# Operand sums moved from GpSimd to VectorE one by one, a reordered seam, and fourth-stage blocks run in pairs

## The chip, the cores and the metric

One Trainium2 core runs the whole program; the metric is the device time of one execution in microseconds (us). The engines are TensorE (PE in the profile, with its weight loads as PEld), VectorE (DVE), ScalarE (ACT), GpSimd (POOL) and SyncE (SP, which here only issues DMAs). TensorE has 128x128 cells; its results go to PSUM, eight banks that VectorE and ScalarE read and GpSimd does not use here.

## The reference, cut to what matters

```python
X = np.fft.rfft(x, axis=1)                       # x: (8, 3072, 256)
Xr, Xi = (X.real.astype(np.float32), X.imag.astype(np.float32))
Yr = Xr @ w_r - Xi @ w_i + b_r                   # mixing over the 256 channels
Yi = Xr @ w_i + Xi @ w_r + b_i
Yr = np.sign(Yr) * np.maximum(np.abs(Yr) - lam, 0.0)      # and Yi alike, lam = 0.01
y = np.fft.irfft(Y, n=x.shape[1], axis=1)
h = y.reshape(B * S, D) @ w_in                   # 256 -> 2048
g = np.where(h >= 1, h, np.where(h <= -1, 0.0, (h + 1) ** 2 / 4))
return g @ w_out                                 # 2048 -> 256
```

## The kernel before

All instructions are issued in an order that is written out by hand (`tc.manual_schedule()`); each engine works through its own list in that order, and semaphores hold an instruction until its inputs are there and its output buffer is free. The kernel has two parts.

**The transform part** runs over `UN` = 96 steps `u`. The forward transform is stages 1 and 2, then comes the mixing (`mix_shared`, `mix_rest`, into a PSUM tile `ps_mix`), bias and threshold (`take_shared` writes `shift`, `add_bias` and `shrink` make `y`, with `over` from ScalarE), and the first inverse stage (`stage3`, tile `ps_i` of L358), whose result goes to memory through `ust`. The last inverse stage (`stage4`) takes it back through `uin`; a block of it is 32 small matmuls in the program (64 in the trace) on quarters of the array, into two PSUM banks. `stage4_out` copies the two banks into the SBUF tile `yt`. Four blocks fill one `yt`.

**The feed-forward part** runs over 32 tiles `i` of 8 units each, 256 units `n` in all (p = n mod 8). The first matrix product is done by a scheme with seven products of half-size blocks instead of eight. Its operands are blocks of `yt` and four differences of such blocks, the operand sums `tsum`, made by `prep_sums(i)` on GpSimd. For accuracy each operand is split into a rounded high part and a low rest (`prep_split_hi` on ScalarE writes `oph`, `prep_split_lo` on VectorE writes `opl`), and each product is three matmuls: high by high, high by low, low by high. In the units p = 4 to 7 of tile i the four parts of the operands of tile i + 1 are split.

A unit runs the seven products into four sum banks X, Z, Y and V. X is read between its products by ScalarE (`snap`). VectorE adds a snapshot to Z, Y or V (`add_floor`, tile `h`, one custom operation). ScalarE squares (`square`, tile `r`), VectorE applies the gate (`gate`, L601), ScalarE rounds (`split_hi`, tile `gh`), VectorE takes the rest (`split_lo`, tile `gl`, L611), and `down` multiplies by `w_out` into the accumulators `acc0` to `acc3`. `output` transposes a finished tile on VectorE (`ot`) in the units p = 0 and 1 of the next tile. So TensorE's stream of unit n holds the products of unit n and the `down` matmuls of units n - 1 and n - 2; there are 45 matmuls of 384 columns in a unit.

The fourth-stage blocks that the feed-forward part needs stand in the units 1, 3, 8 and 10 of each group of 16 units (two tiles), one block at the end of a unit, into the banks V and Y, both copied by ScalarE:

```python
for m, at in enumerate((1, 3, 8, 10)):
    four[(hb - 1) * NK * NP + at] = hb * (JH // JT) + m
...
if n in four:
    stage4(four[n], [bank(k) for k in "VY"])
    stage4_out(four[n], [nc.scalar.copy] * 2)
if i + 1 < NT and p == 3:
    prep_sums(i + 1)
```

There are 14 such groups of 16 units with four blocks each (units 16 to 239); the first group has its blocks in the seam, the last has none. The **seam** is the change from the first part to the second, from about 484 us to 514 us: the last mixing steps, the first operand splits (`prep_split_hi(0, .)` and `prep_split_lo(0, .)`, one part each in the steps u = 95 to 98), the last third-stage sums (into two banks that are copied to the tile `last_u` and stored), two fourth-stage blocks, and the units 0 and 1, where the products of unit 1 can run only as fast as unit 0's snapshots and gates come.

Of the kernel before, what the change touches and what calls it, by code (L numbers as in the profile page):

```python
# [16 lines left out]
P = 128  # L17
# [86 lines left out]
def tile_fft_mix_moe(  # L104
# [408 lines left out]
    def halves_of(i):  # L513
        hb, k = divmod(i, NK)
        y = yt[hb]
        return [[y[:, d, k * QT + t * QT // 2 : k * QT + (t + 1) * QT // 2, :] for t in range(2)] for d in range(ND)]

    def prep_sums(i):
        (b11, b12), (b21, b22) = halves_of(i)
        t = raw_t[i] = pools["in"].tile([P, 4, QT // 2, JH], F32, tag="tsum", name="tsum")  # L520
        for to, a, b in ((0, b12, b11), (2, b22, b12), (1, b22, t[:, 0]), (3, b21, t[:, 1])):
            nc.gpsimd.tensor_tensor(out=t[:, to], in0=a, in1=b, op=ALU.subtract)  # L522


    def split_slices(i, part):
# [72 lines left out]
    def gate(n, f):  # L598
        if 0 <= n < NUNIT:
            h, r = hs[n][:, of(f)], rs[n][:, of(f)]  # L600
            nc.vector.scalar_tensor_tensor(out=h, in0=h, scalar=1.0, in1=r, op0=ALU.max, op1=ALU.min)  # L601
# [70 lines left out]
    with tc.manual_schedule():  # L672
# [69 lines left out]
        for u in range(UN + 3):  # L742
            odd = u % 2
            due.extend(halves(u))
            hs_u = due[: 1 if not odd else max(0, len(due) - 1)]
            del due[: len(hs_u)]
            at = lambda lag: 0 <= u - lag < UN
            weights = more_weights if WU <= u < 85 else lambda: None
            while (stored, 0) in zst:
                store_z(stored)  # L750
                stored += 1
            if at(6) and not odd:
                store_u(u - 6)
            if u == NU:
                wout = keep.tile([P, NF, 2, D], F32R, tag="wout", name="wout")
            if 0 < u < NU - 3:
                load_t(2 * u + 6, 2 * u + 8)
            if 0 < u <= NU:
                load_ti(u - 1)
            if u == WU - 1:  # L760
                load_weights(0)
                load_weights(1)
            if u == 10:
                nc.sync.dma_start(c2_sb, c2)
            if NU <= u + 2 < UN:
                assert stored >= NJ * ((u + 2) // NU + 1)
                load_z(u + 2)
            if xs < min(NH, used + AHEAD):
                load_x(xs)
                xs += 1  # L770
            if at(2):
                mix_shared(u - 2)
            if at(1):
                difference(u - 1)
                rest = split_difference(u - 1)
            if at(2):
                take_shared(u - 2)
            if at(3):
                above(u - 3)
            if at(1):  # L780
                if u > 1:
                    split_X_lo(u - 1)
                rest()
                if u == 1:
                    split_X_lo(u - 1)
                split_first(u - 1)
            if at(3):
                shrink(u - 3)
            weights()
            if at(5) and odd:  # L790
                stage3(u - 5)
            for h in hs_u:
                stage1(h, "AB", [nc.scalar.copy] * 2)
                used += 1
            if u in U4:
                half4()
            weights()
            if u == UN + 1:
                half4("DD")
            if u < UN:  # L800
                stage2(u)
                split_X_hi(u)
            if u == 1:
                filler(2, pools["ps"].tile([P, HT, D], F32, tag="A", name="warm"))
            if at(2):
                mix_rest(u - 2)
                weights()
                add_bias(u - 2)
            if u == U_IN:
                assert not due and stored == NH  # L810
                for _ in ws:
                    pass
                first_st.release()
                pools["in"] = right("in")
                pools["in"].tile([P, 24], F32, name="edge")
                pools["ops0"] = right("ops0")
                for c in range(2):
                    load_u(c)
            if u == UN - 2:
                prep_sums(0)  # L820
            if UN - 1 <= u:
                prep_split_hi(0, u - UN + 1)
                prep_split_lo(0, u - UN + 1)
        mixing.release()
        pools["ops1"] = right("ops1")
        pools["ps"].release()
# [9 lines left out]
        pools["ffg"] = left("ffg")  # L836
        pools["ff"] = left("ff")
        rs[0] = pools["ff"].tile([P, 4, TH], F32, tag="r", name="r")
        last_u = pools["in"].tile([P, 4, QT // 2, JH], F32, tag="tsum", name="last_u").rearrange("p a q j -> p (a q j)")
        last_u = last_u[:, : 4 * D].rearrange("p (k g d) -> p k g d", k=2, g=2)  # L840

        four = {}

        for hb in range(2, NHB):
            for m, at in enumerate((1, 3, 8, 10)):
                four[(hb - 1) * NK * NP + at] = hb * (JH // JT) + m

        for n in range(NUNIT):
            i, p = divmod(n, NP)
            part = p - 4 if i + 1 < NT and p >= 4 else None  # L850

            if n > 0:
                product(n, 1, "X", True)
            snap(n, 1)
            gate(n - 1, 0)
            if n > 0:
                product(n, 2, "Z", True)
            add_floor(n, 1, "Z", 1)
            split_hi(n - 1, 1)
            down(n - 2, 0, 2)  # L860
# [4 lines left out]
            if n == 0:  # L865
# [4 lines left out]
                stage4(c, last4)  # L870
                stage4_out(c, [nc.vector.tensor_copy] * 2)
            split_lo(n - 1, 1)
            output(n - 2, 2)
            split_hi(n - 1, 0)
            down(n - 2, 0, 3)
            if n > 0:
                product(n, 5, "Y", True)
            product(n, 7, "X", False)
            snap(n, 2)
            split_lo(n - 1, 0)  # L880
            if n > 0:
                product(n, 4, "V", True)
            add_floor(n, 2, "Y", 2)
            add_floor(n, 3, "V", 2)
            if n == 0:
                c = next(four4)
                stage4(c, [bank(f"acc{q}") for q in (0, 1)])
            if part is not None:
                prep_split_hi(i + 1, part)
                prep_split_lo(i + 1, part)  # L890
            output(n - 2, 3)
            down(n - 1, 1, 0, 1, 2)
            square(n, 1)
            product(n, 3, "Y", False)
            add_floor(n, 0, "Y", 0)
            down(n - 1, 1, 3)
            if n == 0:
                stage4_out(c, [nc.vector.tensor_copy] * 2)
            square(n, 0)
            gate(n, 1)  # L900
            del snaps[n]
            down(n - 1, 0, 0, 1)
            output(n - 1, 0, 1)
            if n in four:
                stage4(four[n], [bank(k) for k in "VY"])
                stage4_out(four[n], [nc.scalar.copy] * 2)
            if i + 1 < NT and p == 3:
                prep_sums(i + 1)

        n = NUNIT - 1  # L910
        split_hi(n, 1)
# [40 lines left out]
```

## Time and profile before

| | |
|---|---|
| time, median of 3 runs | 2595.58 us (2595.12 to 2596.22) |
| the profiled execution | 2595.19 us, of which the span from first to last instruction is 2593.4 us |
| busy share of the span | PE 99%, PEld 95%, DVE 80%, ACT 65%, POOL 12% |
| clock granted to TensorE | 1.00 in all of the span |
| seam, from the first product (493.10 us) to unit 2 (513.78 us) | 20.68 us, PE busy 17.13 us |
| units 2 to 255 and the end | 2078.92 us, PE busy 2069.70 us |

Busy time of PE is modelled from pipelined matmuls, so its share says that TensorE is nearly always fed, not that each matmul is as fast as it can be. What it loses is read from the starts of its matmuls: two starts that stand further apart than the usual step are lost time. A time in square brackets in a row is the engine's idle time ahead of it and what ended it.

### The profile page before, as it was taken

The numbers are of one execution on the slowest core, as the hardware profiler recorded it, in microseconds if no ns is written. First come the engines' busy times: TensorE is split into PE (matmuls) and PEld (weight loads), VectorE is DVE, ScalarE is ACT, GpSimd is POOL, SyncE is SP. The second block draws the span as 40 slices with busy tenths as digits, with TensorE's granted clock in tenths as the row PEclk, the third lists the DMA queues.
The fourth block names the chain that finished last, engine by engine and source line by source line (L and its number), as shares of the span: only waits on it lengthen the run. The fifth ranks groups of instructions, "written<-read, shape, count | busy, mean of one in ns | idle before, by whom it ended". The sixth has DMA issues, their size and how long they took to land.

```text
span 2593.4 us, 48571 instructions
## 1 busy us (share of the span) xinstructions
PE 2576.4 (99%) x19522; PEld 2459.8 (95%) x19522; DVE 2065.6 (80%) x3120; ACT 1688.5 (65%) x2711; POOL 311.9 (12%) x268
## 2 busy tenths in 40 slices
PE   9999999999999999999999999999999999999998
PEld 7888888899999999999999999999999999999998
DVE  6888866688787878787878787878787878787886
ACT  6777766566666666666666666666666666666665
POOL 4442310100010101010101010101010101010100
PEclk9999999999999999999999999999999999999999
DMA  9988875301111111111111111111111111111001
GB/s 256 277 238 242 237 204 157 109 13 19 26 25 25 25 26 24 27 21 29 18 31 19 29 20 29 20 28 22 26 23 24 25 25 24 25 25 26 13 14 24
DMA packets 194546, 160.31 MB, mean 62 GB/s; under 512 B 117264, under 2 KB 167056, under 8 KB 194320
## 3 DMA queue, kind: packets, MB, share of 16 engines
q1 hardware_dynamic: 192512, 156.73, 24.3%
q8 instruction: 153, 2.51, 0.4%
q10 hardware_dynamic: 1808, 0.48, 0.1%
q14 instruction: 73, 0.60, 0.1%
HBM read 84.78 MB, written 72.35 MB: 61 GB/s over the span
## 4 chain that ended last, share of the span: by engine, by line
PE 92%; DVE 5%; ACT 2%; issue 0%; ACTq 0%
PE acc L623 38%; PE ps_X L567 14%; PE ps_Y L567 10%; PE ps_mix L310 8%; PE ps_V L567 5%; PE ps_Z L567 4%; PE ps_f L254 4%; DVE gl L611 4%; PE ps_i L358 4%; PE ps_i L491 3%; PE ps_f L220 2%; DVE h L586 1%; ACT gh L606 1%; ACT snap L580 1%; PE ps_f L196 1%; ACT yt L506 0%
## 5 line engine op out<-in xcount | busy, mean ns | idle before, releaser
L623 PE MATMUL acc<-gh,wout 128*128 128x384 f32 x4096 | 1204.6, 334 | 0.0
L623 PEld LDWEIGHTS acc<-gh,wout 128*128 128x128 f32 x4096 | 754.2, 188 | 2.4 <-issue 0.8
L596 ACT ACTIVATE r<-h,half 128x768 f32<-128x768 f32 x512 | 480.4, 939 | 385.4 <-DVE h L586 385.3
L623 PE MATMUL acc<-gl,wout 128*128 128x384 f32 x2048 | 684.5, 334 | 1.3 <-DVE gl L611 1.3
L611 DVE TENSOR_TENSOR gl<-h,gh 128x768 fp32r<-128x768 f32 x512 | 529.0, 1038 | 132.5 <-ACT gh L606 105.5
L580 ACT COPY snap<-ps_X 128x384 f32<-128x384 f32 x768 | 369.2, 481 | 286.5 <-PE ps_X L567 286.5
L601 DVE SCALAR_TENSOR_TENSOR h<-h,r 128x768 f32<-128x768 f32 x512 | 504.3, 989 | 29.9
L606 ACT CAST gh<-h 128x768 fp32r<-128x768 f32 x512 | 429.6, 839 | 1.2 <-DVE h L601 1.2
L586 DVE CUSTOM_DVE_ANT_0 h<-ps_Y,snap 128x384 f32<-128x384 f32 x512 | 283.5, 554 | 129.2 <-PE ps_Y L567 129.0
L623 PEld LDWEIGHTS acc<-gl,wout 128*128 128x128 f32 x2048 | 384.5, 188 | 1.9 <-DVE gl L611 1.9
L522 POOL TENSOR_TENSOR tsum<-yt 128x384 f32<-128x384 f32 x64 | 76.1, 1211 | 1931.1 <-ACT yt L506 1357.2
L567 PE MATMUL ps_X<-oph,winh 128*128 128x384 f32 x768 | 263.6, 343 | 1.3 <-ACT snap L580 1.3
L567 PE MATMUL ps_X<-opl,winh 128*128 128x384 f32 x768 | 256.7, 334 | 0.0
L567 PE MATMUL ps_X<-oph,winl 128*128 128x384 f32 x768 | 256.6, 334 | 0.0
L586 DVE CUSTOM_DVE_ANT_0 h<-ps_Z,snap 128x384 f32<-128x384 f32 x256 | 142.4, 556 | 104.9 <-ACT snap L580 104.9
L567 PE MATMUL ps_Y<-oph,winh 128*128 128x384 f32 x512 | 174.5, 341 | 3.3 <-DVE h L586 0.5
L567 PE MATMUL ps_Y<-opl,winh 128*128 128x384 f32 x512 | 171.2, 334 | 0.4 <-DVE opl L544 0.4
L567 PE MATMUL ps_Y<-oph,winl 128*128 128x384 f32 x512 | 171.2, 334 | 0.0
L567 PEld LDWEIGHTS ps_X<-oph,winh 128*128 128x128 f32 x768 | 144.1, 188 | 5.9 <-ACT snap L580 2.5
L340 DVE TENSOR_TENSOR y<-ps_mix,shift 128x512 f32<-128x512 f32 x96 | 66.3, 691 | 99.3 <-PE ps_mix L310 99.0
L567 PEld LDWEIGHTS ps_X<-opl,winh 128*128 128x128 f32 x768 | 144.2, 188 | 0.0
L567 PEld LDWEIGHTS ps_X<-oph,winl 128*128 128x128 f32 x768 | 144.2, 188 | 0.0
(116 smaller groups left out, 3972.3 us busy)
## 6 DMA issues: line engine op xcount, KB each, us to landing
uin<-u_d SPq DMA_DIRECT2D x128, 192.0 KB, 3.4
out<-ot SPq DMA_DIRECT2D x504, 48.0 KB, 2.1
u_d<-ust SPq DMA_DIRECT2D x47, 512.0 KB, 3.7
xin<-in_x SPq DMA_DIRECT2D x112, 192.0 KB, 4.4
z_d<-zst SPq DMA_DIRECT2D x224, 96.0 KB, 2.6
zin<-z_d SPq DMA_DIRECT2D x84, 256.0 KB, 3.8
wraw<-in_moe_w_in SPq DMA_DIRECT2D x16, 256.0 KB, 4.8
wraw<-in_moe_w_out SPq DMA_DIRECT2D x16, 256.0 KB, 4.6
```

The source lines that it names most:

```text
L254: nc.tensor.matmul(ps[:, d, :, gi, :], lhsT=z[:, gi, d * P : (d + 1) * P], rhs=t_sb[:, 2 * v + gi, :].rearrange("p (c s) -> p c s", c=2), ...
L310: nc.tensor.matmul(out, lhsT=a[:, d], rhs=wm[nm, k][:, d, :], start=start and n == 0, stop=n == 3 * ND * len(pairs) - 1, skip_group_check= ...
L358: nc.tensor.matmul(ps[gi][:, k, :], lhsT=ti_sb[rows, v + k, c, :], rhs=y[rows, c, :], start=c == 0 and k == 0, stop=c == 1, tile_position= ...
L491: nc.tensor.matmul(ps[h][cols, d, jj, :], lhsT=a[rows, jj, d * P + e * HP : d * P + (e + 1) * HP], rhs=c2_sb[rows], start=True, stop=True, ...
L567: nc.tensor.matmul(ups[to], lhsT=win[a][p][:, w, :], rhs=mv[:, m, :], start=start and k == 0, stop=k == 2, skip_group_check=True,)
L580: nc.scalar.copy(snaps[n][:, at, :], ups["X"])
L586: nc.vector._custom_dve(TENSOR_ADD_SAT, out=hs[n][:, to, :], in0=ups[a], in1=snaps[n][:, at, :], s0=FLT_MAX, s1=-1.0)
L596: nc.scalar.activation(rs[n][:, of(f)], hs[n][:, of(f)], AF.Square, bias=half, scale=0.5)
L601: nc.vector.scalar_tensor_tensor(out=h, in0=h, scalar=1.0, in1=r, op0=ALU.max, op1=ALU.min)
L606: nc.scalar.copy(gs[n, f][0], hs[n][:, of(f)])
L611: nc.vector.tensor_tensor(out=gl, in0=hs[n][:, of(f)], in1=gh.bitcast(F32), op=ALU.subtract)
L623: nc.tensor.matmul(acc[i, q], lhsT=wout[:, 2 * p + f, a, e * P : (e + 1) * P], rhs=g[:, 1 - t, :], start=p == 0 and f == 1 and k == 0, sto ...
```

## The change

It has three parts.

- **Operand sums.** `prep_sum(i, step, eng)` makes one of the four differences. For tile 0 all four still run on GpSimd; for the other 31 tiles each runs alone on VectorE: steps 0 and 1 in unit p = 3, step 2 in p = 4 and step 3 in p = 5.
- **Seam.** The operand splits of tile 0 stand earlier (part 0 at u = 94, part 1 at 95, parts 2 and 3 at 96), `last_u` takes a buffer of the tile `h` instead of `tsum`, one of the copies of the second fourth-stage block moves to ScalarE, and unit 1 gets an order of its own: four products first, then the squares and gates of unit 0 one at a time, and two `down` parts of unit 0 go from unit 1 to unit 2.
- **Blocks.** The four blocks of a group stand two by two at the ends of the units 2 and 10: the first into X and Z, the second right behind it into V and Y. The last of the four copies is held until after the first snapshot of the next unit.

```diff
--- before.py
+++ after.py
@@ -515,11 +515,17 @@
         y = yt[hb]
         return [[y[:, d, k * QT + t * QT // 2 : k * QT + (t + 1) * QT // 2, :] for t in range(2)] for d in range(ND)]
 
+    def prep_sum(i, step, eng):
+        (b11, b12), (b21, b22) = halves_of(i)
+        if step == 0:
+            raw_t[i] = pools["in"].tile([P, 4, QT // 2, JH], F32, tag="tsum", name="tsum")
+        t = raw_t[i]
+        to, a, b = ((0, b12, b11), (1, b22, t[:, 0]), (2, b22, b12), (3, b21, t[:, 1]))[step]
+        eng.tensor_tensor(out=t[:, to], in0=a, in1=b, op=ALU.subtract)
+
     def prep_sums(i):
-        (b11, b12), (b21, b22) = halves_of(i)
-        t = raw_t[i] = pools["in"].tile([P, 4, QT // 2, JH], F32, tag="tsum", name="tsum")
-        for to, a, b in ((0, b12, b11), (2, b22, b12), (1, b22, t[:, 0]), (3, b21, t[:, 1])):
-            nc.gpsimd.tensor_tensor(out=t[:, to], in0=a, in1=b, op=ALU.subtract)
+        for step in range(4):
+            prep_sum(i, step, nc.gpsimd)
 
 
     def split_slices(i, part):
@@ -818,9 +824,9 @@
                     load_u(c)
             if u == UN - 2:
                 prep_sums(0)
-            if UN - 1 <= u:
-                prep_split_hi(0, u - UN + 1)
-                prep_split_lo(0, u - UN + 1)
+            for part in {UN - 2: (0,), UN - 1: (1,), UN: (2, 3)}.get(u, ()):
+                prep_split_hi(0, part)
+                prep_split_lo(0, part)
         mixing.release()
         pools["ops1"] = right("ops1")
         pools["ps"].release()
@@ -836,25 +842,34 @@
         pools["ffg"] = left("ffg")
         pools["ff"] = left("ff")
         rs[0] = pools["ff"].tile([P, 4, TH], F32, tag="r", name="r")
-        last_u = pools["in"].tile([P, 4, QT // 2, JH], F32, tag="tsum", name="last_u").rearrange("p a q j -> p (a q j)")
+        last_u = pools["ff"].tile([P, 4, TH], F32, tag="h", bufs=2, name="last_u").rearrange("p a n -> p (a n)")
         last_u = last_u[:, : 4 * D].rearrange("p (k g d) -> p k g d", k=2, g=2)
 
-        four = {}
+        four, later, held = {}, [], []
 
         for hb in range(2, NHB):
-            for m, at in enumerate((1, 3, 8, 10)):
+            for m, at in ((0, 2), (2, 10)):
                 four[(hb - 1) * NK * NP + at] = hb * (JH // JT) + m
 
         for n in range(NUNIT):
             i, p = divmod(n, NP)
             part = p - 4 if i + 1 < NT and p >= 4 else None
+            step = {3: 0, 4: 2, 5: 3}.get(p) if i + 1 < NT else None
 
             if n > 0:
                 product(n, 1, "X", True)
             snap(n, 1)
-            gate(n - 1, 0)
+            if held:
+                nc.scalar.copy(*held.pop())
+            if n != 1:
+                gate(n - 1, 0)
             if n > 0:
                 product(n, 2, "Z", True)
+            if n == 1:
+                product(n, 5, "Y", True)
+                product(n, 4, "V", True)
+            if n == 2:
+                down(0, 0, 0, 1)
             add_floor(n, 1, "Z", 1)
             split_hi(n - 1, 1)
             down(n - 2, 0, 2)
@@ -870,42 +885,62 @@
                 stage4(c, last4)
                 stage4_out(c, [nc.vector.tensor_copy] * 2)
             split_lo(n - 1, 1)
+            if n == 1:
+                square(0, 0)
+                gate(0, 0)
             output(n - 2, 2)
-            split_hi(n - 1, 0)
+            if step is not None:
+                prep_sum(i + 1, step, nc.vector)
+            if n != 1:
+                split_hi(n - 1, 0)
             down(n - 2, 0, 3)
-            if n > 0:
+            if n > 1:
                 product(n, 5, "Y", True)
             product(n, 7, "X", False)
             snap(n, 2)
-            split_lo(n - 1, 0)
-            if n > 0:
+            if n == 1:
+                split_hi(0, 0)
+            else:
+                split_lo(n - 1, 0)
+            if n > 1:
                 product(n, 4, "V", True)
             add_floor(n, 2, "Y", 2)
             add_floor(n, 3, "V", 2)
             if n == 0:
                 c = next(four4)
                 stage4(c, [bank(f"acc{q}") for q in (0, 1)])
+                stage4_out(c, [nc.scalar.copy, lambda *a: later.append(a)])
+            if n == 1:
+                split_lo(0, 0)
             if part is not None:
                 prep_split_hi(i + 1, part)
                 prep_split_lo(i + 1, part)
+            if step == 0:
+                prep_sum(i + 1, 1, nc.vector)
             output(n - 2, 3)
             down(n - 1, 1, 0, 1, 2)
+            if n == 1:
+                down(n - 1, 1, 3)
             square(n, 1)
             product(n, 3, "Y", False)
             add_floor(n, 0, "Y", 0)
-            down(n - 1, 1, 3)
+            if n != 1:
+                down(n - 1, 1, 3)
             if n == 0:
-                stage4_out(c, [nc.vector.tensor_copy] * 2)
-            square(n, 0)
+                nc.vector.tensor_copy(*later.pop())
+            else:
+                square(n, 0)
             gate(n, 1)
             del snaps[n]
-            down(n - 1, 0, 0, 1)
+            if n > 1:
+                down(n - 1, 0, 0, 1)
             output(n - 1, 0, 1)
             if n in four:
-                stage4(four[n], [bank(k) for k in "VY"])
-                stage4_out(four[n], [nc.scalar.copy] * 2)
-            if i + 1 < NT and p == 3:
-                prep_sums(i + 1)
+                c = four[n]
+                stage4(c, [bank(k) for k in "XZ"])
+                stage4_out(c, [nc.scalar.copy] * 2)
+                stage4(c + 1, [bank(k) for k in "VY"])
+                stage4_out(c + 1, [nc.scalar.copy, lambda *a: held.append(a)])
 
         n = NUNIT - 1
         split_hi(n, 1)
```

ScalarE's list around a block, in units 26 and 27 of the program (`yt<-ps_i` are the copies of a block, `snap` the copies of bank X, `r` the squares, `gh` the rounding), before:

```order
L596 ACTIVATE r<-h,half 128x768 x2
L506 COPY yt<-ps_i_9136 128x96x4
L506 COPY yt<-ps_i_9137 128x96x4
L580 COPY snap<-ps_X 128x384
L606 CAST gh<-h 128x768
L580 COPY snap<-ps_X 128x384
L606 CAST gh<-h 128x768
```

and of the change:

```order
L602 ACTIVATE r<-h,half 128x768 x2
L506 COPY yt<-ps_i_9097 128x96x4
L506 COPY yt<-ps_i_9098 128x96x4
L506 COPY yt<-ps_i_9136 128x96x4
L586 COPY snap<-ps_X 128x384
L863 COPY yt<-ps_i_9137 128x96x4
L612 CAST gh<-h 128x768
L586 COPY snap<-ps_X 128x384
L612 CAST gh<-h 128x768
```

Three copies now stand ahead of the first snapshot of the unit behind a block, and the fourth between it and the first rounding. VectorE's list in units 27 and 28 (p = 3 and the start of p = 4) before, where no sum stands in it (`h<-ps_Z`, `h<-ps_Y` and `h<-ps_V` are `add_floor`):

```order
L586 ISA h<-ps_Z,snap 128x384
L611 TENSOR_TENSOR gl<-h,gh 128x768 x2
L586 ISA h<-ps_Y,snap 128x384
L586 ISA h<-ps_V,snap 128x384
L586 ISA h<-ps_Y,snap 128x384
L601 SCALAR_TENSOR_TENSOR h<-h,r 128x768 x2
```

and of the change:

```order
L592 ISA h<-ps_Z,snap 128x384
L617 TENSOR_TENSOR gl<-h,gh 128x768
L524 TENSOR_TENSOR tsum<-yt 128x384
L617 TENSOR_TENSOR gl<-h,gh 128x768
L592 ISA h<-ps_Y,snap 128x384
L592 ISA h<-ps_V,snap 128x384
L524 TENSOR_TENSOR tsum<-yt,tsum 128x384
L592 ISA h<-ps_Y,snap 128x384
L607 SCALAR_TENSOR_TENSOR h<-h,r 128x768 x2
L592 ISA h<-ps_Z,snap 128x384
L617 TENSOR_TENSOR gl<-h,gh 128x768
L524 TENSOR_TENSOR tsum<-yt 128x384
```

The first sum of a unit stands between the two `gl` operations, the second of p = 3 between the `add_floor` of V and the last `add_floor` of Y. In the seam VectorE's list, at the last mixing steps (`y`, `shift` and `Xd` belong to the mixing, `opl` is an operand's low part), reads before:

```order
L544 TENSOR_TENSOR opl<-yt,oph 128x384
L285 TENSOR_TENSOR Xd<-ps_f_6721,Xd 128x256
L326 TENSOR_TENSOR shift<-ps_mix,bias_i 128x256
L296 TENSOR_TENSOR Xl<-ps_f_6721,Xh 128x512
L303 TENSOR_TENSOR Xdl<-Xd,Xdh 128x256
L349 SCALAR_TENSOR_TENSOR y<-y,over 128x512
L340 TENSOR_TENSOR y<-ps_mix,shift 128x512
L544 TENSOR_TENSOR opl<-yt,oph 128x768
```

and of the change:

```order
L550 TENSOR_TENSOR opl<-yt,oph 128x768
L285 TENSOR_TENSOR Xd<-ps_f_6725,Xd 128x256
L326 TENSOR_TENSOR shift<-ps_mix,bias_i 128x256
L296 TENSOR_TENSOR Xl<-ps_f_6725,Xh 128x512
L303 TENSOR_TENSOR Xdl<-Xd,Xdh 128x256
L349 SCALAR_TENSOR_TENSOR y<-y,over 128x512
L340 TENSOR_TENSOR y<-ps_mix,shift 128x512
L550 TENSOR_TENSOR opl<-tsum,oph 128x768 x2
```

Each split stands one mixing step earlier, so that a wider one now stands ahead of `shift` of the step u = 96.

## Rows read from the trace of the kernel before

**Rows 1.** Page, busy time of each engine: us, share of the span, instructions.

```profile
PE 2576.4 (99%) x19522; PEld 2459.8 (95%) x19522; DVE 2065.6 (80%) x3120; ACT 1688.5 (65%) x2711; POOL 311.9 (12%) x268
```

**Rows 2.** Timeline, first product of units 64, 69, 70 and 80: start, us, engine, line.

```profile
1016.03 0.33 PE L567 MATMUL ps_X<-oph,winh 128*128 128x384 f32 x1
...
1058.09 0.33 PE L567 MATMUL ps_X<-oph,winh 128*128 128x384 f32 x1
...
1065.89 0.33 PE L567 MATMUL ps_X<-oph,winh 128*128 128x384 f32 x1
...
1146.82 0.33 PE L567 MATMUL ps_X<-oph,winh 128*128 128x384 f32 x1
```

**Rows 3.** Timeline of PE, the block at the end of unit 74 (unit 10 of its group).

```profile
1105.83 0.33 PE L623 MATMUL acc<-gl,wout 128*128 128x384 f32 x1
1106.00 0.34 PE L623 MATMUL acc<-gh,wout 128*128 128x384 f32 x1
1106.27 1.15 PE L491 MATMUL ps_i<-c_sb,uin 48*64 48x48 f32 x64
1107.35 0.45 PE L567 MATMUL ps_X<-oph,winh 128*128 128x384 f32 x1
1107.63 0.34 PE L567 MATMUL ps_X<-opl,winh 128*128 128x384 f32 x1
```

**Rows 4.** Timeline of POOL, DVE and PEld in unit 75 (unit 11 of its group).

```profile
1108.40 1.99 POOL L522 TENSOR_TENSOR tsum<-yt 128x384 f32<-128x384 f32 x2 [87.73 <-ACT yt L506]
1110.34 3.44 POOL L522 TENSOR_TENSOR tsum<-yt,tsum 128x384 f32<-128x384 f32 x2
...
1109.48 3.42 DVE L611 TENSOR_TENSOR gl<-h,gh 128x768 fp32r<-128x768 f32 x2
...
1113.43 0.19 PEld L567 LDWEIGHTS ps_Y<-oph,winh 128*128 128x128 f32 x1 [0.40 <-DVE h L586]
```

**Rows 5.** All waits of the span: who for whom, us, times, longest.

```profile
PEld ps_Y L567 <- DVE h L586: 13.3, 32, 0.8
```

**Rows 6.** Timeline of DVE and PE in unit 74, where POOL is idle.

```profile
1101.90 0.96 DVE L611 TENSOR_TENSOR gl<-h,gh 128x768 fp32r<-128x768 f32 x1 [0.55 <-ACT gh L606]
1102.78 0.55 DVE L586 CUSTOM_DVE_ANT_0 h<-ps_Y,snap 128x384 f32<-128x384 f32 x1
1103.24 0.55 DVE L586 CUSTOM_DVE_ANT_0 h<-ps_V,snap 128x384 f32<-128x384 f32 x1
1104.81 0.56 DVE L586 CUSTOM_DVE_ANT_0 h<-ps_Y,snap 128x384 f32<-128x384 f32 x1 [1.02 <-PE ps_Y L567]
...
1104.09 0.33 PE L567 MATMUL ps_Y<-oph,winh 128*128 128x384 f32 x1
```

**Rows 7.** Groups by form: count, busy us, mean ns of one, idle before.

```profile
L544 DVE TENSOR_TENSOR opl<-yt,oph 128x384 fp32r<-128x384 f32 x32 | 17.6, 549 | 0.2 <-ACT oph L540 0.2
```

**Rows 8.** Timeline of ACT behind the block of unit 74.

```profile
1107.47 0.86 ACT L506 COPY yt<-ps_i 128x384 f32<-128x384 f32 x2 [1.12 <-PE ps_i L491]
1108.23 0.48 ACT L580 COPY snap<-ps_X 128x384 f32<-128x384 f32 x1
1108.61 0.84 ACT L606 CAST gh<-h 128x768 fp32r<-128x768 f32 x1
```

**Rows 9.** Timeline of PE in the seam.

```profile
486.24 0.38 PE L310 MATMUL ps_mix<-wm_bh,Xh 128*128 128x256 f32 x1 [0.44 <-DVE shift L326]
...
494.14 0.34 PE L567 MATMUL ps_Y<-oph,winh 128*128 128x384 f32 x1
...
497.13 2.00 PE L358 MATMUL ps_i<-y,ti_sb 64*128 64x256 f32 x16
...
505.58 0.44 PE L567 MATMUL ps_X<-oph,winh 128*128 128x384 f32 x1 [0.92 <-ACT snap L580]
...
509.43 0.44 PE L623 MATMUL acc<-gl,wout 128*128 128x384 f32 x1 [0.65 <-DVE gl L611]
...
511.57 0.44 PE L567 MATMUL ps_Y<-oph,winh 128*128 128x384 f32 x1 [0.47 <-DVE h L586]
```

## Prediction

> **What bounds the kernel now.** I read the page first: TensorE is busy for 2576.4 of 2593.4 us, VectorE for 80% of the span [rows 1]. A busy share says nothing on the pace, so I then went to the timeline for the starts of TensorE's matmuls. A unit in which nothing is in the way takes 1065.89 - 1058.09 = 7.80 us from its first product to the next unit's. A whole group of 16 units takes 1146.82 - 1016.03 = 130.79 us [rows 2], where 16 x 7.80 would be 124.80. So TensorE's stream of full matmuls is the bound, and the change can only take away what lies between them: 5.99 us in each group, and what is lost in the seam.
>
> Of those 5.99 us the blocks are the larger share. At a block the last `acc` matmul starts at 1106.00 and the next product at 1107.35: 1.35 us where the step is 0.17 (1105.83 to 1106.00), and the second matmul behind it comes 0.28 later instead of 0.17. A block costs 1.18 + 0.11 = 1.29 us: 0.10 at the entry (0.27 to its first matmul instead of 0.17), 1.08 for itself up to the next product, 0.11 behind [rows 3]. Four of them are 5.16 us. The remaining 0.83 us must be waits. The view of all waits has them: the weights of a product into Y wait for VectorE 32 times, 13.3 us in all, longest 0.8 [rows 5], two per group in 16 groups and 0.83 us per group. Where they come from is seen in unit 75: GpSimd makes the operand sums from 1108.40 to 1113.78, and VectorE's two `gl`, 0.96 us each where GpSimd rests [rows 6], fill 3.42 us without a pause. The `add_floor` that frees Y comes late, and Y's weights wait 0.40 us [rows 4].
>
> **The change part by part.**
>
> *Sums leave GpSimd.* After tile 0 no GpSimd work is left beside VectorE, so the stretched `gl` should go back to 0.96 us and the 32 waits should vanish: -13.3 us.
>
> *Sums on VectorE.* This adds 31 x 4 = 124 operations of 384 elements on operands in SBUF. The nearest row is the low part of the same size: 549 ns [rows 7]. Two such operations back to back start 0.46 apart (1102.78 and 1103.24), so one takes 0.46 to 0.55 us of the queue, 57 to 68 us over the run. What hides it: ahead of the second `gl` VectorE idles 0.55 us for ScalarE's rounding, and there stands the first sum of each of the units p = 3, 4 and 5. The second sum of p = 3 stands ahead of the last `add_floor`, where VectorE idles 1.02 us for the product into Y. In p = 4 and 5 that second gap already holds a split, and the sum does not touch it. Should the first sum run over by 0.1 us, the `add_floor` of Y, which ends at 1102.78 + 0.55 = 1103.33, still has 0.76 us before TensorE wants the bank at 1104.09 [rows 6]. I cost the sums at nothing. Without these gaps they cost up to 2.2 us a tile.
>
> *Blocks in pairs.* Of the two blocks the first pays entry and exit as now, 1.29 us. No row shows a second one right behind. From above it costs 1.29 us, if it pays both again or waits for its banks; from below 0.97, if of the 1.08 us another 0.11 belongs to the way back to full-width products. I take 1.00, near the lower end, because both blocks use the same shapes and the banks V and Y are long free (the last `add_floor` of Y ends at 1105.37 in unit 74, the block starts at 1106.27 [rows 3, 6]). That is -0.29 us for each of 28 pairs: -8.1 us; bounds 0 and -9.0.
> [...]
>
> Behind the pair ScalarE is the one to watch. It takes 0.12 us after a block to begin, then 0.86 for two copies [rows 8]. X and Z are thus free 0.98 us after the first block's end, within the second block, and the next unit's X finds its bank. The copy of V takes 0.12 + 0.48 = 0.60 us after the second block; the first snapshot starts 0.88 us after the block even now (1108.23 - 1107.35), so it is not late. The held copy of Y then stands ahead of the rounding `gh` and shifts it by one step of ScalarE, 0.38 us (1108.23 to 1108.61). `gl`, the sum and the second `gl` move by about as much, and of the 0.76 us ahead of Y some 0.36 is left. Nothing is lost, but this is the tightest place.
>
> *Seam.* Now TensorE goes from its first product into Y at 494.14 to the third stage at 497.13: 2.99 us for six steps of 0.17, so 1.95 us are lost on low parts that come late. With all splits three steps earlier this goes. Against it, the split ahead of `shift` in step 96 is 768 wide instead of 384: 0.96 against 0.55 on VectorE, 0.84 against 0.48 on ScalarE (the times of `gl`, the small `opl`, the rounding and a snapshot [rows 6 to 8]), so the wait of 0.44 us at 486.24 grows by up to 0.77. And the third stage may then wait up to 0.4 for the last `y`, an estimate. Left: -0.8. In the units 0 and 1 the waits of 0.92, 0.65 and 0.47 us make 2.04 [rows 9]. The new order puts two products of unit 1 ahead of the first of them and splits the squares, but one snapshot still stands behind a rounding of 0.84 us; with that left over, -1.2. Refilling behind a wait costs 0.11 as behind a block, for some four waits another -0.5. I take -2.5 us in all; bounds 0, if the waits only change places, and -4.9, if all of 1.95 + 0.44 + 2.04 and the refills go.
>
> *Nothing else moves onto the path.* The loads `uin` for a pair are issued 8 units, some 62 us, ahead of use. The copies are as many as before.
>
> *Sum:* 13.3 + 8.1 + 2.5 = 23.9 us. From the profiled execution's 2595.19 that is 2571.3; the median of the runs shown is 0.39 higher, which gives 2571.7, and I say 2571.5 us.
>
> **The rivals.**
>
> *The pairs and the seam give nothing* (the second block waits at its banks or pays entry and exit again, seam waits only move). For it: the unmeasured price and a hand-counted seam. Against it: the shapes are equal and the banks free. Both at nothing: 2595.6 - 13.3 = 2582.3; half of both 2577.
>
> *The waits at Y stay*, because GpSimd is not what stretches VectorE; then the first part does not do what it says, and 2595.6 - 8.1 - 2.5 = 2585.0. For it: only that two things coincide. Against it: `gl` is 0.96 us in unit 74 and 1.7 in unit 75, and GpSimd is what differs.
>
> *Slower: the sums come onto the path.* The place is the first sum of a tile, between the two `gl` and ahead of the `add_floor` that frees Y, in p = 3 behind a pair, and then again in p = 4 and 5. All that VectorE does behind it comes later, and TensorE waits at Y. Its price in full is four operations of 0.55 us in 31 tiles, 68 us, which would give 2640. It decides from 23.9 / 31 = 0.77 us per tile, a third of the added work, and is slower by more than the measurement tells from no change from 0.94 us. For it: VectorE is already at 80%, and ScalarE's held copy eats into the same 0.76 us. Against it: 0.55 and 1.02 us of idle time at exactly these places.
> [...]
>
> **How the numbers follow.** The forecast, 2568 to 2576, has 0.74; the first rival (2576 to 2584) 0.14; the waits that stay (2584 to 2590) 0.04; sums partly on the path, so that it comes out within 0.2% (2590.4 to 2600.8), 0.04; slower 0.04. A change of 0.2%, 5.2 us, is about what a measurement of this kernel can tell from none. So faster 0.92, same 0.04, slower 0.04. The range goes down to all bounds taken at once, 13.3 + 9.0 + 4.9 = 27.2 us, less 1 us for the spread of the runs: 2567.5. Upwards it reaches the first rival in full: 2582.5.
>
> **What would show it.** GpSimd has no `tsum` after the first four; the mean of `gl` falls to about 960 ns; the wait of Y's weights for VectorE falls from 13.3 us to under 1. Between the last `acc` and the first product a pair takes about 0.27 + 1.08 + 1.00 = 2.35 us. A group takes 124.8 + 2 x 2.29 = 129.4 us instead of 130.8. Unit 3 starts about 2.5 us earlier than now. I am wrong if products into Y wait in p = 3 to 5, if the first snapshot behind a pair comes more than 0.9 us after it, or if the seam shows new waits at the mixing.

## The result, and the profile after

The change makes the kernel 1.0% faster: 2570.03 us (median of 4 runs, 2569.27 to 2570.22) against 2595.67 us (2595.12 to 2596.22), ratio 0.9898 with a 95% interval of 0.9883 to 0.9913. The prediction was 2571.5 us with a range of 2567.5 to 2582.5. The profiled execution took 2570.20 us, its span is 2568.4 us.

The page's line of busy times after the change:

```profile
PE 2555.3 (99%) x19522; PEld 2460.9 (96%) x19522; DVE 2058.8 (80%) x3243; ACT 1692.1 (66%) x2712; POOL 135.5 (5%) x144
```

TensorE has the same 19522 matmuls and is busy for 21.1 us less [rows 1]. VectorE has 123 operations more and still 6.8 us less busy time (the page counts overlapping operations once). That is not because of the sums: with them alone on VectorE its busy time is 2065.4 us, as before, so they add about as much as GpSimd's work had stretched the rest. The drop comes with the pairs, which alone give 2051.8 us; why is not shown. The groups by form have what was stretched, `gl` and the gate, first before, then of the change (count, busy us, mean ns of one, idle before):

```profile
L611 DVE TENSOR_TENSOR gl<-h,gh 128x768 fp32r<-128x768 f32 x512 | 529.0, 1038 | 132.5 <-ACT gh L606 105.5
L601 DVE SCALAR_TENSOR_TENSOR h<-h,r 128x768 f32<-128x768 f32 x512 | 504.3, 989 | 29.9
```

```profile
L617 DVE TENSOR_TENSOR gl<-h,gh 128x768 fp32r<-128x768 f32 x512 | 488.6, 954 | 113.4 <-ACT gh L612 85.4
L607 DVE SCALAR_TENSOR_TENSOR h<-h,r 128x768 f32<-128x768 f32 x512 | 486.6, 950 | 31.8 <-ACT r L602 0.3
...
L524 DVE TENSOR_TENSOR tsum<-yt,tsum 128x384 f32<-128x384 f32 x62 | 34.1, 550 | 0.0
```

`gl` takes 954 ns on average, as the prediction had it, and a sum 550 ns, as its nearest row did [rows 7]. The view of all waits, in which the weights of Y waited 32 times for VectorE [rows 5], has this left:

```profile
PEld ps_Y L573 <- DVE h L592: 0.2, 1, 0.2
```

Where TensorE's time went is read from the starts of its matmuls: the seam from the fourth-stage block of step 96 to the first product of unit 3, then the first product of unit 64, the pair at the end of unit 74, Y's third product in unit 75, the first product of unit 80.

```profile
484.50 1.15 PE L491 MATMUL ps_i<-c_sb,uin 48*64 48x48 f32 x64
486.81 0.38 PE L310 MATMUL ps_mix<-wm_bh,Xh 128*128 128x256 f32 x1 [1.16 <-DVE shift L326]
...
494.71 0.33 PE L573 MATMUL ps_Y<-oph,winh 128*128 128x384 f32 x1
...
495.85 2.00 PE L358 MATMUL ps_i<-y,ti_sb 64*128 64x256 f32 x16
...
505.54 0.44 PE L573 MATMUL ps_X<-oph,winh 128*128 128x384 f32 x1 [0.62 <-ACT snap L586]
...
517.63 0.33 PE L573 MATMUL ps_X<-oph,winh 128*128 128x384 f32 x1
...
1006.97 0.33 PE L573 MATMUL ps_X<-oph,winh 128*128 128x384 f32 x1
...
1094.85 0.34 PE L629 MATMUL acc<-gh,wout 128*128 128x384 f32 x1
1095.12 2.14 PE L491 MATMUL ps_i<-c_sb,uin 48*64 48x48 f32 x128
1097.19 0.44 PE L573 MATMUL ps_X<-oph,winh 128*128 128x384 f32 x1
...
1103.05 0.33 PE L573 MATMUL ps_Y<-oph,winh 128*128 128x384 f32 x1
...
1136.33 0.33 PE L573 MATMUL ps_X<-oph,winh 128*128 128x384 f32 x1
```

A group of 16 units takes 1136.33 - 1006.97 = 129.36 us instead of 130.79 [rows 2]. The pair stands between 1094.85 and 1097.19: 2.34 us, where one block took 1.35 [rows 3]. So the second block costs 0.99 us, or 1.29 - 0.99 = 0.30 us less than a single one. In the seam the wait for low parts ahead of the third stage is gone (494.71 to 495.85 is 1.14 us instead of 2.99 [rows 9]), the wait for `shift` has grown from 0.44 to 1.16 us, as forecast, and of the waits in units 0 and 1 one of 0.62 us is left. In the trace of before the first and the fifth of these rows read:

```profile
484.65 1.15 PE L491 MATMUL ps_i<-c_sb,uin 48*64 48x48 f32 x64
...
521.58 0.33 PE L567 MATMUL ps_X<-oph,winh 128*128 128x384 f32 x1
```

Unit 3 starts at 517.63 instead of 521.58. But the trace is already 0.15 us ahead at the block of step 96, so the seam itself went from 521.58 - 484.65 = 36.93 to 517.63 - 484.50 = 33.13 us: 3.80 us.

How the sums lie in VectorE's list in unit 75, the tightest place of the prediction (p = 3 behind a pair):

```profile
1099.72 0.96 DVE L617 TENSOR_TENSOR gl<-h,gh 128x768 fp32r<-128x768 f32 x1 [0.49 <-ACT gh L612]
1100.59 0.55 DVE L524 TENSOR_TENSOR tsum<-yt 128x384 f32<-128x384 f32 x1
1101.06 0.95 DVE L617 TENSOR_TENSOR gl<-h,gh 128x768 fp32r<-128x768 f32 x1
1101.93 0.55 DVE L592 CUSTOM_DVE_ANT_0 h<-ps_Y,snap 128x384 f32<-128x384 f32 x1
1102.40 0.55 DVE L592 CUSTOM_DVE_ANT_0 h<-ps_V,snap 128x384 f32<-128x384 f32 x1
1102.86 0.55 DVE L524 TENSOR_TENSOR tsum<-yt,tsum 128x384 f32<-128x384 f32 x1
1103.77 0.56 DVE L592 CUSTOM_DVE_ANT_0 h<-ps_Y,snap 128x384 f32<-128x384 f32 x1 [0.36 <-PE ps_Y L573]
```

The first sum takes 0.47 us of the queue (1100.59 to 1101.06) in a gap that the rounding leaves. The `add_floor` of Y ends at 1102.48, and TensorE's next product into Y starts at 1103.05 without a wait: 0.57 us to spare. The second sum lies in the idle time ahead of the last `add_floor`, of which 0.36 us is still left. The first snapshot behind the pair starts at 1098.09, 0.90 us after the product at 1097.19, just at the limit that the prediction had named; ScalarE stands idle for 0.31 us there until the product is done, so it is not late.

### The profile page after: what moved, and what is told of

Same layout as the page of the kernel before. It is cut to its first block, busy times and chain, and to the rows that moved or that the text cites. A ratio compares the mean times of both kernels' runs of the same rounds, so it can differ in the third digit from the quotient of the medians.

```text
span 2568.4 us, 48565 instructions
## 1 busy us (share of the span) xinstructions
PE 2555.3 (99%) x19522; PEld 2460.9 (96%) x19522; DVE 2058.8 (80%) x3243; ACT 1692.1 (66%) x2712; POOL 135.5 (5%) x144
## 4 chain that ended last, share of the span: by engine, by line
PE 98%; DMA 1%; DVE 0%; POOL 0%; ACT 0%; issue 0%; SPq 0%
PE acc L629 41%; PE ps_X L573 16%; PE ps_Y L573 10%; PE ps_mix L310 8%; PE ps_Z L573 5%; PE ps_V L573 5%; PE ps_f L254 4%; PE ps_i L358 4%; PE ps_i L491 2%; PE ps_f L220 2%; DMA wm_sti<-in_w_i 0%; DMA xin<-in_x_first 0%; DVE h L607 0%; DVE h L592 0%; POOL wm_al L165 0%
## 5 line engine op out<-in xcount | busy, mean ns | idle before, releaser
L617 DVE TENSOR_TENSOR gl<-h,gh 128x768 fp32r<-128x768 f32 x512 | 488.6, 954 | 113.4 <-ACT gh L612 85.4
L607 DVE SCALAR_TENSOR_TENSOR h<-h,r 128x768 f32<-128x768 f32 x512 | 486.6, 950 | 31.8 <-ACT r L602 0.3
L592 DVE CUSTOM_DVE_ANT_0 h<-ps_V,snap 128x384 f32<-128x384 f32 x256 | 139.7, 546 | 0.0
```

Source lines behind the costliest of these rows:

```text
L592: nc.vector._custom_dve(TENSOR_ADD_SAT, out=hs[n][:, to, :], in0=ups[a], in1=snaps[n][:, at, :], s0=FLT_MAX, s1=-1.0)
L617: nc.vector.tensor_tensor(out=gl, in0=hs[n][:, of(f)], in1=gh.bitcast(F32), op=ALU.subtract)
```

## The experiments

First come the three parts, each alone, and the question of the engine; then the room that the sums stand in and two details of the pairs; then the seam. The runs of the kernel before that stood beside them had medians of 2595.62, 2595.92 and 2596.01 us.

**The sums alone on VectorE.** The kernel before with this edit:

```diff
+            step = {3: 0, 4: 2, 5: 3}.get(p) if i + 1 < NT else None
...
+            if step is not None:
+                prep_sum(i + 1, step, nc.vector)
...
+            if step == 0:
+                prep_sum(i + 1, 1, nc.vector)
...
-            if i + 1 < NT and p == 3:
-                prep_sums(i + 1)
```

> The kernel before with the first part alone: the four sums of the tiles 1 to 31 on VectorE, in the units p = 3, 4 and 5; blocks and seam as before. Theory (the sums are hidden, GpSimd's work beside VectorE was the cause of the waits at Y): about 13 us faster, 2582 us, the wait of Y's weights for VectorE under 1 us, gl near 955 ns. Rival (part of the gain needs the other parts, since blocks now stand in the same units 3 and 11 as sums): 2586 to 2590 us, with waits at Y in these units.

Measured: 2581.69 us, ratio 0.9947 (0.9933 to 0.9962), 13.9 us faster. Its view of waits:

```profile
PEld ps_Y L573 <- DVE h L592: 0.2, 1, 0.2
```

The theory holds: the waits at Y and the time went together, `gl` is at 956 ns, and the sums cost nothing that shows. Part of the gain lies in the seam, although its order is the old one:

```profile
485.31 1.15 PE L491 MATMUL ps_i<-c_sb,uin 48*64 48x48 f32 x64
...
520.54 0.33 PE L573 MATMUL ps_X<-oph,winh 128*128 128x384 f32 x1
```

That is 35.23 us from the block of step 96 to unit 3, 1.70 less than before. The waits of 0.65 us for `gl` and of 0.47 us at Y in the seam [rows 9] are gone: before, GpSimd made the sums of tile 1 beside just these units:

```profile
505.55 3.00 POOL L522 TENSOR_TENSOR tsum<-yt 128x384 f32<-128x384 f32 x2 [27.23 <-ACT snap L580]
508.52 3.39 POOL L522 TENSOR_TENSOR tsum<-yt,tsum 128x384 f32<-128x384 f32 x2
```

So two of the 32 waits at Y, 0.79 and 0.21 us by the weight loads, belong to the seam; the other 30 are 12.3 us, and the sums gave 13.9 - 1.7 = 12.2 us outside the seam.

**The pairs alone.**

```diff
-            for m, at in enumerate((1, 3, 8, 10)):
+            for m, at in ((0, 2), (2, 10)):
...
-                stage4(four[n], [bank(k) for k in "VY"])
-                stage4_out(four[n], [nc.scalar.copy] * 2)
+                c = four[n]
+                stage4(c, [bank(k) for k in "XZ"])
+                stage4_out(c, [nc.scalar.copy] * 2)
+                stage4(c + 1, [bank(k) for k in "VY"])
+                stage4_out(c + 1, [nc.scalar.copy, lambda *a: held.append(a)])
```

The held copy stands behind the next unit's first snapshot, as in the change.

> The kernel before with the blocks in pairs alone; sums on GpSimd, seam as before. Theory (a second block right behind costs 0.95 us instead of 1.29): 28 x 0.34 = 9.5 us faster, 2586 us, the waits at Y stay near 13 us. Rival (behind a pair the held copy and GpSimd's sums of unit 11 meet, so the wait at Y of that unit grows by up to 0.4 us, and some of the gain is lost): 2589 to 2592 us, waits at Y of 17 us or more.

Measured: 2583.31 us, ratio 0.9954 (0.9939 to 0.9969), 12.3 us faster, 2.8 us more than the theory had, and against the rival. Its waits:

```profile
PEld ps_Y L567 <- DVE h L586: 10.1, 32, 0.8
```

The waits at Y fell by 3.2 us although GpSimd still makes the sums. What is left, 12.3 - 3.2 = 9.1 us, is the pairs' own. The timeline shows why the wait in unit 11 of a group got shorter:

```profile
1107.00 2.84 DVE L611 TENSOR_TENSOR gl<-h,gh 128x768 fp32r<-128x768 f32 x2 [0.49 <-ACT gh L606]
...
1106.31 2.71 POOL L522 TENSOR_TENSOR tsum<-yt 128x384 f32<-128x384 f32 x2 [87.85 <-ACT yt L856]
```

GpSimd waits for the held copy (L856), starts its sums later against the unit, and the two `gl` are stretched to 2.84 us instead of 3.42 [rows 4]. So these two parts overlap: together they should win some 3 us less than the sum of each alone. The run below with the sums on GpSimd agrees: on top of the pairs and the seam the sums are worth 9.7 us, not 13.9.

**The seam alone.** The changed kernel with the sums back on GpSimd and the blocks single, as before.

> The kernel before with the seam's new order alone; sums on GpSimd, blocks singly. Theory (the seam's gain is its own): 3 to 4 us faster, 2592 us. Rival (the seam gains from VectorE being free of GpSimd's sums of tile 1, which now would run beside it): 1 us or less, 2594.5 to 2595.7 us.

Measured: 2592.27 us, ratio 0.9987 (0.9977 to 0.9996), 3.35 us faster. The theory holds: from the block of step 96 to unit 3 this trace has 33.14 us, as the change has. But 1.7 us of it is the gain that the sums alone have too, reached in another way. Here GpSimd still makes the sums of tile 1, but earlier, and it is done before the units 0 and 1 need VectorE:

```profile
492.06 2.42 POOL L522 TENSOR_TENSOR tsum<-yt 128x384 f32<-128x384 f32 x2 [12.87 <-DVE opl L544]
```

By the edit `last_u` no longer takes the buffer of `tsum`, and the splits that read it are earlier; in the run of the pairs alone the profile names the storing of `last_u` as what these sums waited 27.5 us for, until 506.25. So I take the free buffer for the cause of the earlier start; no run has it alone. The three parts alone make 13.9 + 12.3 + 3.4 = 29.6 us; less the overlaps of 3.2 (sums and pairs) and 1.7 (sums and seam) it is 24.7, where the change measured 25.6. The runs of one kernel spread by 0.8 to 2.9 us here, so this is about as near as the medians can come.

**The single sums on GpSimd.** The same places in the written order, another engine:

```diff
-                prep_sum(i + 1, step, nc.vector)
+                prep_sum(i + 1, step, nc.gpsimd)
...
-                prep_sum(i + 1, 1, nc.vector)
+                prep_sum(i + 1, 1, nc.gpsimd)
```

> The changed kernel, but the single sums are issued on GpSimd instead of VectorE, at the same places of the written order. Theory (the engine decides: GpSimd has nothing else in its list, so it runs all four together as soon as the data is there, wherever they stand, and stretches VectorE): the waits at Y come back, some 13 us slower than the changed kernel, 2583 us. Rival (it is the place in the order and the spreading that help): within 3 us of the changed kernel, 2570 to 2573 us.

Measured: 2579.69 us, 9.7 us slower than the changed kernel. The view of waits and GpSimd's timeline in unit 75:

```profile
PEld ps_Y L573 <- DVE h L592: 9.5, 31, 0.4
```

```profile
1101.85 1.02 POOL L524 TENSOR_TENSOR tsum<-yt 128x384 f32<-128x384 f32 x1 [87.81 <-ACT yt L863]
1102.95 1.61 POOL L524 TENSOR_TENSOR tsum<-yt,tsum 128x384 f32<-128x384 f32 x1
1104.52 1.73 POOL L524 TENSOR_TENSOR tsum<-yt 128x384 f32<-128x384 f32 x1
1106.20 1.02 POOL L524 TENSOR_TENSOR tsum<-yt,tsum 128x384 f32<-128x384 f32 x1
```

The engine decides, not the place: GpSimd's list holds nothing else, so the four sums run together as soon as the last copy is there, or, for the other tile of a group, as soon as the last low part has freed their buffer. The size is 9.7 and not 13, because the pairs shorten the same waits, as in the experiment on them.

**Each sum twice and three times.** The repetition writes the same result again.

```diff
-        eng.tensor_tensor(out=t[:, to], in0=a, in1=b, op=ALU.subtract)
+        for _ in range(2 if i else 1):
+            eng.tensor_tensor(out=t[:, to], in0=a, in1=b, op=ALU.subtract)
```

> The changed kernel with each of the 124 sums on VectorE done twice (the same result written again), to see how much room they stand in. Theory (the gaps of 0.55 and 1.02 us and the 0.76 us ahead of Y hide them): 57 to 68 us more work for VectorE, but at most 3 us slower than the changed kernel, 2570 to 2573 us; if at all, TensorE waits at Y in the units 3 and 11 behind a pair, by about 0.1 us. Rival (VectorE's room is used up by the first four sums): a quarter or more of the added work shows, 2585 us or more, with waits at Y in p = 3, 4 and 5.

> The same with each sum done three times, 115 to 136 us more work for VectorE than in the changed kernel. Theory: the first gap is overrun by 0.87 us, 0.1 us more than the 0.76 us ahead of Y, and by 0.5 us behind a pair, so waits at Y appear in p = 3, 4 and 5: 2580 to 2595 us. Rival (VectorE has room to spare far beyond these gaps): under 2574 us. Rival (all of it is paid): 2685 us or more.

Measured: 2576.17 us with two, 2640.24 us with three. The first is 6.1 us slower than the changed kernel, more than the 3 us that I allowed; the second 70 us, far above the range. The waits at Y, with two:

```profile
PEld ps_Y L574 <- DVE h L593: 6.8, 29, 0.2
```

and with three:

```profile
PEld ps_Y L574 <- DVE h L593: 64.8, 94, 0.8
```

With two sums, 28 of the 29 waits, of 0.2 us each, stand in the units 3 and 11 behind a pair, as the theory has it, only larger: a repeated sum starts 0.59 us after the first, not 0.46; why was not tested by itself. With three, 93 of the 94 waits are three for each of the 31 tiles, in p = 3, 4 and 5 (in both runs one wait of 0.2 us is the seam's). The timeline of VectorE shows what I had not counted, that there is nothing left to catch up in (unit 68, p = 4):

```profile
1062.01 0.95 DVE L618 TENSOR_TENSOR gl<-h,gh 128x768 fp32r<-128x768 f32 x1
1062.88 1.74 DVE L525 TENSOR_TENSOR tsum<-yt 128x384 f32<-128x384 f32 x3
1064.53 0.95 DVE L618 TENSOR_TENSOR gl<-h,gh 128x768 fp32r<-128x768 f32 x1
1065.40 0.55 DVE L593 CUSTOM_DVE_ANT_0 h<-ps_Y,snap 128x384 f32<-128x384 f32 x1
```

No idle time is left in front of any of them, so a unit hands its delay on to the next. Room for the sums is there once, and not quite twice. Of some 146 us that three instead of one add (248 x 0.59) 70 us show; from two to three it is 64 of some 73 us.

**Both blocks of a pair in two banks.**

```diff
-                stage4(c, [bank(k) for k in "XZ"])
+                stage4(c, [bank(k) for k in "VY"])
```

> The changed kernel with both blocks of a pair in the banks V and Y, so that the second must wait until ScalarE has copied the first. Theory (the pairs need the four banks, since TensorE works in order and has nothing else to do there): 0.12 + 0.86 us of wait in each of 28 pairs and the entry paid again, some 30 us slower than the changed kernel, 2600 us, slower than the kernel before. Rival (the first of the two copies frees enough, or the wait overlaps with the block): 2580 us or less.

Measured: 2602.55 us, ratio 1.0025 (1.0016 to 1.0035): 32.5 us slower than the changed kernel. Its timeline at the second block of the pair of unit 74:

```profile
1105.27 1.52 PE L491 MATMUL ps_i<-c_sb,uin 48*64 48x48 f32 x64 [0.58 <-ACT yt L506]
1106.72 0.45 PE L573 MATMUL ps_X<-oph,winh 128*128 128x384 f32 x1
```

The second block waits 0.58 us for V's copy and then runs 1.52 us instead of 1.15, since its matmuls alternate between V and Y and Y is copied later (its weight loads wait another 0.19 us behind the first two). 32.5 / 28 = 1.16 us a pair. The theory holds: pairing without the two further banks would have lost more than all that the change won.

**The last copy not held.**

```diff
-                stage4_out(c + 1, [nc.scalar.copy, lambda *a: held.append(a)])
+                stage4_out(c + 1, [nc.scalar.copy] * 2)
```

> The changed kernel with the last copy of a pair not held: ScalarE copies Y right behind V, ahead of the next unit's first snapshot. Theory (a single copy of 0.38 us a step fits before the snapshot's inputs are there, 0.98 against 0.88 us behind the block): within 1 us of the changed kernel, 2570 to 2571 us. Rival (holding it is what keeps the snapshot in time): the product that waits for the snapshot stands 0.1 to 0.4 us in each of 28 units, 2573 to 2582 us.

Measured: 2569.26 us (2568.45 to 2569.87). No difference beyond the spread: holding the copy is not needed.

**The splits of tile 0 as before, and a better place for one of them.** The changed kernel once more ran beside both, on the same chip.

```diff
-            for part in {UN - 2: (0,), UN - 1: (1,), UN: (2, 3)}.get(u, ()):
-                prep_split_hi(0, part)
-                prep_split_lo(0, part)
+            if UN - 1 <= u:
+                prep_split_hi(0, u - UN + 1)
+                prep_split_lo(0, u - UN + 1)
```

> The changed kernel with the operand splits of tile 0 back in the steps of before (u = 95 to 98); the new order of the units 0 and 1 stays. Theory (the earlier splits trade 1.95 us of late low parts for a longer wait at shift, 1.1 us of the seam's gain is theirs, the rest belongs to the units 0 and 1): about 1.1 us slower than the changed kernel; from the first mixing wait to the third stage as before, the wait at shift back at 0.44 us. Rival (the seam's gain hangs on the splits, since the units 0 and 1 start later without them): 3 us or more slower.

The other leaves the splits where the change has them, but for the low part of part 1 (and does not hold the copy):

```diff
                 prep_split_hi(0, part)
-                prep_split_lo(0, part)
+                if part != 1:
+                    prep_split_lo(0, part)
...
+            if u == UN:
+                prep_split_lo(0, 1)
             if at(3):
                 shrink(u - 3)
```

> The changed kernel with two small edits: in step 96 the low part of the operand part 1 stands behind shift and the mixing's own low parts instead of ahead of them, and the last copy of a pair isn't held. Theory (the 1.16 us wait of the mixing for shift is made by that one operation's place): the wait goes, about 1.2 us for it and 0.5 us for the copy, 1 to 2 us faster than the changed kernel, about 2568.5 us. Rival (shift is late for its own inputs, or the third stage then waits for the last y): no difference, 2569 to 2570 us.

> The changed kernel once more, to stand beside the two others on the same chip. All theories: 2570 us within 1 us.

Measured: 2571.98 us (2571.39 to 2572.07) with the old splits, 2568.80 us (2567.86 to 2569.32) with the moved low part, 2569.35 us (2568.97 to 2569.51) for the change. The runs with the old splits lie 2.63 us above the change by their medians, and the two don't overlap; in the profiled executions the spans are 2568.7 and 2567.3 us, 1.4 us apart, and the rest lies outside the first and the last instruction. So I read the sizes from the traces, from the block of step 96 to the first product behind the third stage. The change again:

```profile
484.81 1.15 PE L491 MATMUL ps_i<-c_sb,uin 48*64 48x48 f32 x64
487.12 0.39 PE L310 MATMUL ps_mix<-wm_bh,Xh 128*128 128x256 f32 x1 [1.16 <-DVE shift L326]
...
498.09 0.44 PE L573 MATMUL ps_X<-oph,winh 128*128 128x384 f32 x1
```

With the old splits:

```profile
484.81 1.15 PE L491 MATMUL ps_i<-c_sb,uin 48*64 48x48 f32 x64
486.40 0.39 PE L310 MATMUL ps_mix<-wm_bh,Xh 128*128 128x256 f32 x1 [0.44 <-DVE shift L326]
...
499.22 0.44 PE L573 MATMUL ps_X<-oph,winh 128*128 128x384 f32 x1
```

With the moved low part:

```profile
484.35 1.15 PE L491 MATMUL ps_i<-c_sb,uin 48*64 48x48 f32 x64
485.43 0.39 PE L310 MATMUL ps_mix<-wm_bh,Xh 128*128 128x256 f32 x1
...
496.40 0.44 PE L573 MATMUL ps_X<-oph,winh 128*128 128x384 f32 x1
```

These are 13.28, 14.41 and 12.05 us. In the seam the earlier splits are worth 1.13 us, as the theory said; what the times of whole runs have beyond that stays open. Behind `shift` the low part of part 1 costs nothing: the wait of 1.16 us is gone and nothing takes its place, 1.23 us better than the change in the trace. In the times of whole runs its median is 0.55 us lower, within their spread, so that this version beats the changed kernel is shown by the trace of the seam alone.

## Why the prediction was right

- **The waits at Y** were forecast at -13.3 us. The wait fell from 13.3 to 0.2 us. That GpSimd's sums were the cause is shown by putting them back on GpSimd: 9.5 us of waits stand there again. But the prediction's "two per group in 16 groups" was misread: two of the 32 waits, 1.0 us, lie in the seam, and the longer one it counted a second time, as the 0.47 us at Y among the seam's waits. Outside the seam the term is 12.3 us, and the sums alone gave 12.2 there. Not forecast was that the pairs shorten these waits too, by 3.2 us; where the sums have left GpSimd, that part is not there to be won twice.
- **The sums on VectorE at nothing**: right, by the gaps that the prediction named. Of the 0.76 us ahead of Y behind a pair 0.57 was left, where I had said 0.36. The tests with more sums show that the slower rival was a real one, with its place and its mechanism: with each sum tripled the waits at Y make the kernel slower than before. Its price in full was not reached: about half of the added work shows then.
- **The pairs** were forecast at -8.1 us by a second block of 1.00 us. It is 0.99 in the row of unit 74, 28 x 0.30 = 8.4 us; the pairs alone gave 9.1 without the waits. If only entry and exit were saved, a pair would gain 0.10 + 0.11 = 0.21 us by the rows of before [rows 3]; the runs show 0.30, so more than these two goes, and what it is was not shown.
- **The seam** was forecast at -2.5 us and is the term that was mis-sized: alone it gave 3.35, and the traces show 3.80 from the block of step 96 to unit 3. The splits are 1.13 of it (forecast 0.8). Here 1.85 of the 1.95 us of late low parts went, `shift` waits 0.72 us longer (I had up to 0.77), and there is no wait for the last `y`, for which I had put 0.4. (The splits stand one step earlier, the last one two, not three as I wrote.) The other 2.68 us are the units 0 and 1, forecast at 1.7. Here the cause was partly wrong: I put all the waits down to the order of the instructions, and two of them, 0.65 and 0.47 us, came from GpSimd's sums of tile 1, as the run with the sums alone shows by losing them, 1.70 us in all. The size was wrong for two more reasons: I overlooked a fourth wait, of 0.39 us for a snapshot at 507.28, and the waits cost more than their brackets. The one of 0.92 us stands in a gap of 505.58 - 504.32 = 1.26 us where the step is 0.17, and the second matmul behind it comes 0.28 us later (505.86) instead of 0.17, another 0.11: 1.20 us. Where I wrote that 0.8 us would stay, the one of 0.62 stayed.
- **The sum**: 12.3 + 8.4 + 3.8 = 24.5 us, against 25.0 between the profiled spans and 25.6 between the medians. That the forecast of 23.9 came so near is in part luck: the waits at Y were counted 1.0 us too high and the seam 1.3 us too low.

## What to carry to other kernels

Where one engine is nearly always fed, look for what makes its feeders late, not for what they are busy with: here work on an otherwise idle GpSimd stretched VectorE's operations by about as much as the same work costs VectorE itself (40 us of `gl` and 18 us of the gate, against 124 x 0.47 = 58 us), and did so where TensorE had to wait for it (13.3 us). The moved work cost nothing that shows as long as it fitted the gaps of the list it was moved to, so place it by the idle times of that engine and check how long the next reader can wait; here the gaps held the sums once, and each repetition showed in the time (6.1 us with two, 64 us more with three). An operation can also be in the way far from where one looks: two waits that seemed to belong to the order of the seam, of 0.65 and 0.47 us, were GpSimd's. The blocks of small matmuls on parts of the array were cheaper side by side, with banks for all of them (0.99 us for the second block, where a single one costs 1.29; with two banks for both the change was 32.5 us slower).

## What the runs showed of the hardware

In unit 75 of the kernel before, GpSimd's four differences of 384 elements took 1.02, 1.02, 1.75 and 1.61 us. The first ran beside an `add_floor` of 0.56 us, the other three beside the two `gl`, which took 1.73 and 1.77 us there, where one takes 0.96 us while GpSimd is idle [rows 6]. So both `gl` and two of the three differences beside them were longer; why the second was not is not shown. With the single sums on GpSimd the four took 1.02 to 1.73 us. No view of the profile names this, since both engines only show as busy. In the runs with repeated sums, a sum that writes what the one before has just written started 0.59 us after it, where two `add_floor` operations, into different data, start 0.46 apart [rows 6].
